# A planned order for GpSimd on the port it shares with VectorE, and another table of stage settings

## The chip, the cores and the metric

One core of a Trainium2 chip. The time is the device time of one execution in microseconds (us). Executions of one kernel agree within about 0.3%. Ratios are the mean time of one kernel's fast runs over that of the kernel before in the same rounds, so they are not quite the ratios of the medians that are quoted beside them. A ratio of 0.99 is 7.8 us.

## The reference

A gated sum of an attention block (32 heads of 16, sequence 2048, width 512) and of a block of two small MLPs:

```python
x = A_x
g = _sigmoid((x * gate_w).sum(-1, keepdims=True))
a = _A_ref(x, A_wqkv, A_wo)              # softmax attention
b = _B_ref(x, B_w1, B_w2, B_w3, B_w4)    # layernorm, GELU, shifted channels; layernorm, GELU
return g * a + (1 - g) * b
```

The exponentials of attention are the bulk: 2048 tiles of 128 x 512.

## The kernel before

The kernel doesn't fix its instruction order by hand. A small model of the engines runs while the program is built (the *planner*); the order in which it starts jobs is the order in which instructions are put into each engine's program. Engines then run freely: each takes its own instructions in order and waits only for data and buffers.

```python
def try_engine(self, e):                      # the planner: engine e is free
    ...
        if any(not self.free[b.cls] for b in j.acq) or j.port and self.lock > self.t:
            continue                          # a job that uses the shared port waits for it
    ...
    self.emit(self.t, j.fn)                   # its place in the program
    self.t_free[e] = self.t + j.hold
    if j.port:
        self.lock = self.t + j.hold           # the port is taken, in the model
```

So the planner knows that VectorE and GpSimd share a port, and never lets two port jobs overlap. But nothing in the program enforced it: the chip could run a GpSimd job earlier against VectorE than planned.

A tile's exponential is made on ScalarE (two tiles in one instruction), or on VectorE with integer arithmetic: one pass from PSUM for each tile, then three shifted copies of a pair of tiles. Two copies usually fall to VectorE, the third to GpSimd:

```python
def sh(k=k):
    d = [b.slot for b in bufs]
    if alone or k == 1 or k == 2 and not both:
        nc.vector.tensor_scalar(out=d[k][:, 0:w], in0=d[0][:, 0:w], scalar1=float(SHIFT * k), scalar2=None,
                                op0=ALU.add)
    else:
        nc.gpsimd.tensor_scalar(out=d[k][:, 0:w], in0=d[0 if both else 2][:, 0:w], scalar1=1.0, ...)
```

A table `STAGES` overrides two dozen settings of the planner for each 32 tiles (how far to look ahead, when VectorE stops taking tiles, how many matmuls fit a gap, `GP2` and `GP3` for the share of copies on GpSimd).

The softmax here doesn't subtract the row's maximum and nothing guards it: scores larger than these inputs give would overflow.

Of the kernel before, what the change touches and what calls it, by code (L numbers as in the profile page):

```python
# [11 lines left out]
ALU = mybir.AluOpType  # L12
# [7 lines left out]
SHIFT = 32  # L20
# [69 lines left out]
class Sim:  # L90
# [45 lines left out]
    def emit(self, t, fn):  # L136
        if fn is not None:
            self.n += 1
            self.order.append((t, self.n, fn))

    def finish_job(self, job):
        job.done = self.t
        self.release(job.frees)

    def try_engine(self, e):
        if self.t_free[e] > self.t:
            return False
        best = None
        for j in self.jobs[e]:
            if j.at > self.tiles:  # L150
                continue
            if j.ready is None:
                if any(d.done is None for d in j.deps):
                    continue
                j.ready = self.t
            if any(not self.free[b.cls] for b in j.acq) or j.port and self.lock > self.t:
                continue
            key = (j.prio, j.ready, j.seq)
            if best is None or key < best[0]:
                best = (key, j)  # L160
        if best is None:
            return False
        j = best[1]
        self.jobs[e].remove(j)
        for b in j.acq:
            self.take(b)
        j.start = self.t
        self.emit(self.t, j.fn)
        self.t_free[e] = self.t + j.hold
        if j.port:  # L170
            self.lock = self.t + j.hold
        self.busy[e] += j.hold
        self.log.append((e, self.t, j.hold, j.name))
        self.push(self.t + j.hold, None)
        self.pending -= 1
        self.push(self.t + j.hold + j.lat, lambda: self.finish_job(j))
        return True
# [57 lines left out]
def kernel(  # L235
# [14 lines left out]
    nc = tc.nc  # L250
# [35 lines left out]
        P1_PRIO=0.414,  # L286
        S_PRIO=0.38,
        GP2=0.0,
        GP3=1.0,
        DVE_STOP=6,  # L290
        DVE_STOP_L=8,
        URG=5,
        URG_L=17,
        DVE_ALONE=2,
        EARLY=68,
        SL=(45, 60),
        IDLE_NS=537,
        PD_LOW=0,
        PA_LOW=0,
        DVE_WAIT=3,  # L300
        AHEAD=9,
        AHEAD2=9,
        PV_FULL=0.916,
        PV_IDLE=0.37,
        PRESS=27,
        MAXU=9,
        ROT=0, DUE_SH=0, AT_SH=0,
    )
    SEG = 32
    STAGES = {0: {'AHEAD': 6, 'EARLY': 13, 'DVE_ALONE': 150, 'S_PRIO': 0.368}, 1: {'AHEAD': 8, 'S_PRIO': 0.415}, 2: {'ROT': 3, 'URG': 3, 'MAXU': 9, 'PD_LOW': 3}, 3: {'PA_LOW': 3, 'DVE_WAIT': 4}, 4: {'SL': (25, 60), 'URG': 2, 'DVE_STOP_L': 9, 'DUE_SH': 40}, 5: {'SL': (25, 60), 'URG': 2, 'DVE_STOP_L': 9, 'DUE_SH': 40}, 6: {'S_PRIO': 0.234}, 7: {'PRESS': 17, 'DVE_WAIT': 5}, 8: {'PV_FULL': 0.776, 'AHEAD': 7, 'PD_LOW': 0}, 9: {'PV_FULL': 0.877, 'ROT': 2, 'AHEAD': 6, 'PA_LOW': 0}, 10: {'PV_FULL': 0.794, 'PA_LOW': 0, 'SL': (165, 60), 'DVE_ALONE': 2}, 11: {'SL': (85, 100), 'EARLY': 62}, 12: {'EARLY': 124, 'PV_IDLE': 0.433, 'DVE_STOP_L': 11, 'SL': (25, 40)}, 13: {'GP3': 0.6, 'DVE_ALONE': 150}, 14: {'ROT': 3, 'GP3': 0.9, 'URG_L': 16, 'AHEAD2': 12}, 15: {'P1_PRIO': 0.309, 'DVE_STOP_L': 5, 'AT_SH': 60, 'DVE_STOP': 5}, 16: {'DVE_WAIT': 2, 'AHEAD2': 10}, 17: {'ROT': 1, 'AT_SH': 10, 'GP3': 0.8, 'DVE_ALONE': 2}, 18: {'P1_PRIO': 0.403, 'GP2': 0.2}, 19: {'PRESS': 10}, 20: {'URG': 7, 'AT_SH': 60, 'GP2': 0.2}, 21: {'IDLE_NS': 352, 'DVE_ALONE': 300}, 22: {'S_PRIO': 0.257}, 23: {'PRESS': 52, 'AT_SH': 60}, 24: {'PA_LOW': 3, 'PRESS': 23, 'GP3': 0.8}, 25: {'PV_IDLE': 0.414, 'AT_SH': 10}, 26: {'DUE_SH': 8, 'PD_LOW': 1, 'GP2': 0.2, 'GP3': 0.9}, 28: {'AHEAD2': 10, 'EARLY': 142}, 29: {'AHEAD': 8, 'S_PRIO': 0.388, 'GP3': 0.9, 'ROT': 1}, 30: {'PV_IDLE': 0.372, 'DUE_SH': -40, 'S_PRIO': 0.412, 'PA_LOW': 2}, 31: {'IDLE_NS': 311, 'GP3': 0.9, 'P1_PRIO': 0.22}, 32: {'DUE_SH': 40, 'DVE_STOP': 5}, 33: {'DVE_STOP_L': 7, 'SL': (205, 60)}, 34: {'P1_PRIO': 0.326, 'PD_LOW': 0, 'PV_IDLE': 0.37, 'GP2': 0.35}, 36: {'PD_LOW': 1, 'DVE_STOP': 7}, 37: {'URG': 4, 'IDLE_NS': 589}, 38: {'ROT': 2}, 39: {'EARLY': 155, 'PA_LOW': 3}, 40: {'DUE_SH': -20, 'PRESS': 8}, 41: {'P1_PRIO': 0.584, 'PA_LOW': 3, 'MAXU': 10}, 42: {'AHEAD2': 8, 'PRESS': 58, 'DVE_ALONE': 0}, 43: {'PD_LOW': 0, 'DVE_WAIT': 2, 'P1_PRIO': 0.216, 'PV_FULL': 1}, 44: {'MAXU': 7, 'ROT': 1}, 45: {'PRESS': 10, 'SL': (65, 80)}, 46: {'DVE_WAIT': 6, 'AT_SH': 120, 'PD_LOW': 0}, 47: {'DUE_SH': 80, 'P1_PRIO': 0.59, 'DVE_ALONE': 150, 'AHEAD2': 6}, 48: {'URG': 8, 'AT_SH': 120}, 49: {'PD_LOW': 3, 'ROT': 3, 'DVE_WAIT': 6, 'AT_SH': 120}, 50: {'DVE_WAIT': 1, 'SL': (5, 60), 'GP2': 0.35, 'DVE_STOP_L': 11}, 51: {'PA_LOW': 3, 'URG_L': 18}, 52: {'ROT': 2, 'PD_LOW': 1, 'PRESS': 35}, 53: {'URG_L': 16, 'IDLE_NS': 245, 'PRESS': 19}, 54: {'PD_LOW': 3}, 56: {'MAXU': 10, 'GP2': 0.1}, 57: {'URG': 2}, 58: {'ROT': 3, 'DVE_WAIT': 5}, 59: {'ROT': 1}, 60: {'GP2': 0.2, 'PV_FULL': 0.879, 'SL': (85, 100)}, 61: {'GP3': 0.6, 'GP2': 0.35, 'PV_FULL': 0.985}, 62: {'GP3': 0.6, 'GP2': 0.35, 'PV_FULL': 0.985}}  # L310
    K = SimpleNamespace(**BASE)


# [11 lines left out]
    def slots(name, n, shape, dt=BF16, where=const):  # L325
# [58 lines left out]
        "den": slots("den", 3, [4, 512], F32, dpool),  # L384
        "rr": slots("rr", 3, [4, 512], F32, dpool),
    })

    def dve(hold, deps, fn, **kw):
        return sim.add(Job("DVE", hold, 280.0, deps, fn, **kw))
# [32 lines left out]
    issue = {"SP": 740.0}  # L422
# [66 lines left out]
    for j in range(4):  # L489
        dma(2200.0, [j_wl], lambda j=j: nc.sync.dma_start(  # L490
            out=woL[32 * j + 1:32 * j + DH + 1, :], in_=A_wo[(25 + 2 * j) * DH:(26 + 2 * j) * DH, :]), prio=5)
# [3 lines left out]
    def warm_pe():  # L495
        for _ in range(11):
# [4 lines left out]
                                                            op0=ALU.bitwise_and), prio=0)  # L501
# [446 lines left out]
    def close_pair(pr):  # L948
        evs["pair"] = None
        evs["n"] = evs.get("n", 0.0) + K.GP2  # L950
        both = evs["n"] >= 1.0
        if both:
            evs["n"] -= 1.0
        rl = pr["pv"][0][0]
        alone = n_left(rl) <= (K.URG_L if rl == NR - 1 else K.URG)
        evs["m"] = evs.get("m", 0.0) + 1.0 - K.GP3
        if evs["m"] >= 1.0:
            evs["m"] -= 1.0
            alone = True
        both = both and not alone  # L960
        w = 512 * pr["h"]
        bufs = [pr["buf"]] + [Buf("PD", pr["h"] + (k == 2)) for k in range(1, 4)]
        pr["buf"].users = pr["h"] + (3 if both or alone else 2)
        bufs[2].users = pr["h"] + (0 if both or alone else 1)
        last = list(pr["jobs"])
        chain = [last]
        for k in range(1, 4):
            def sh(k=k):
                d = [b.slot for b in bufs]
                if alone or k == 1 or k == 2 and not both:  # L970
                    nc.vector.tensor_scalar(out=d[k][:, 0:w], in0=d[0][:, 0:w], scalar1=float(SHIFT * k), scalar2=None,  # L971
                                            op0=ALU.add)
                else:
                    nc.gpsimd.tensor_scalar(out=d[k][:, 0:w], in0=d[0 if both else 2][:, 0:w], scalar1=1.0,  # L974
                                            scalar2=float(SHIFT * (k if both else 1)), op0=ALU.mult, op1=ALU.add)
            if alone or k == 1 or k == 2 and not both:
                j = dve(0.26 * w + 72.0, pr["jobs"], sh, prio=K.S_PRIO, acq=[bufs[k]], frees=[bufs[0]], port=True)
            else:
                j = gp(0.833 * w + 165.0, pr["jobs"] if both else last, sh, prio=1, acq=[bufs[k]],
                       frees=[bufs[0 if both else 2]])  # L980
            if k == 3:
                j.frees.append(pr["token"])
            last = [j]
            chain.append(last)
        for h2, (r2, kt2, i2, G2, p2) in enumerate(pr["pv"]):
            for k in range(4):
                hd = 8 * G2 + 2 * i2 + p2
                V = (lambda kt=kt2, hd=hd: V0[:, kt, hd, :]) if k < 2 else (lambda kt=kt2, hd=hd: V2[:, kt // 2, hd, :])
                add_pv(r2, i2, kt2, V, lambda h2=h2, b=bufs[k]: b.slot[:, h2 * 512:(h2 + 1) * 512].bitcast(BF16),
                       list(chain[k]) + [j_v[kt2, G2 // 2] if k < 2 else j_v2[kt2, G2 // 2]], bufs[k])  # L990
# [371 lines left out]
```

## Time and profile before

782.44 us, the median of 3 runs (782.32 to 783.42).

| in the trace of before | |
|---|---|
| tiles on ScalarE / on VectorE | 1483 / 565 |
| shifted copies on VectorE / on GpSimd | 579 / 270 |
| VectorE instructions on the shared port that took over 60 ns more than usual ("stalls") | 38, 26.2 us too long |
| of these, behind a GpSimd instruction planned *later* ("inverted") | 31, 24.2 us |
| GpSimd jobs that start before the last port instruction of VectorE planned ahead of them has ended | 67 |

How to read it: all three main engines are busy 95% or more, so a busy share says little; what tells is who waits for whom, and whether a wait was planned. The stalls lie inside VectorE's records, which only get longer; the rows of the table come from going through all records and laying the planned order beside them. The lines of the profile are in the prediction. In them, psA and ring are tiles of scores in PSUM, the memory that matmuls write; PA and PD are the exponentials that ScalarE and VectorE make of them; acc is the sum that matmuls build from these.

### The profile page before, as it was taken

To read this page: it belongs to the slowest core of one execution; us is meant where nothing else is said; L and a number is where in the kernel's file an instruction comes from. 1 tells how busy PE (TensorE), PEld (TensorE's weight loads), DVE (VectorE), ACT (ScalarE), POOL (GpSimd) and SP (SyncE) were. 2 spreads that over 40 slices of the span, in tenths; PEclk is the share of its full clock that TensorE was granted. 3 is DMA by queue.
4 is the path that set the end of the run, shared out by engine and by line. 5 is a ranking of instruction groups with operands and counts; after the bars stand their busy time and mean duration, and the time that the engine had idled before them with its cause. 6 is when DMAs were issued, how large, how long until landed. Compare 5 with 4: busy or idle time off the path is not lost.

```text
span 781.1 us, 23746 instructions
## 1 busy us (share of the span) xinstructions
PE 765.1 (98%) x9588; PEld 227.1 (29%) x9588; DVE 740.0 (95%) x1575; ACT 744.4 (95%) x767; POOL 341.5 (44%) x332
## 2 busy tenths in 40 slices
PE   9999999999999999999999999999999999999997
PEld 5333322222222222223232223222223222223222
DVE  6999999999999999998989999999999899999996
ACT  6899999999999999999989999999999999999996
POOL 2255534443344444344345444343454444455531
PEclk9999999999999999999999999999999999999999
DMA  9402133132001221142001001001100000000001
GB/s 191 139 3 37 52 99 84 45 75 86 3 19 33 60 70 39 45 126 50 23 18 33 23 20 47 23 26 25 42 19 20 22 15 26 27 19 20 8 20 40
DMA packets 67093, 34.60 MB, mean 44 GB/s; under 512 B 46748, under 2 KB 62380, under 8 KB 66984
## 3 DMA queue, kind: packets, MB, share of 16 engines
q1 hardware_dynamic: 66040, 32.56, 16.4%
q8 instruction: 75, 1.23, 0.7%
q10 hardware_dynamic: 944, 0.52, 0.2%
q14 instruction: 34, 0.28, 0.1%
HBM read 17.40 MB, written 6.81 MB: 31 GB/s over the span
## 4 chain that ended last, share of the span: by engine, by line
PE 54%; DVE 29%; ACT 10%; issue 4%; DMA 1%; SPq 0%; DVEq 0%; ACTq 0%
PE acc L1005 19%; PE psA L829 17%; PE ring L519 16%; DVE PD L935 12%; DVE PD L971 10%; ACT PA L909 6%; ACT hB L753 2%; ACT hT L753 2%; DVE x_sb L731 1%; DVE st L662 1%; PE ring L829 1%; DVE xn L682 1%; DVE hB L752 1%; DVE accsb L1021 1%; ACT L909 1%
## 5 line engine op out<-in xcount | busy, mean ns | idle before, releaser
L909 ACT ACTIVATE PA<-psA 128x1024 bf16<-128x1024 f32 x742 | 694.5, 1040 | 23.1 <-PE psA L829 8.5
L974 POOL TENSOR_SCALAR PD<-PD 128x1024 uint16<-128x1024 uint16 x270 | 285.1, 1059 | 403.7 <-DVE PD L971 256.6
L935 DVE TENSOR_SCALAR PD<-ring 128x512 uint16<-128x512 f32 x565 | 372.6, 680 | 23.4 <-PE ring L829 21.6
L1005 PE MATMUL acc<-PD,V 128*17 128x512 bf16 x2260 | 308.9, 381 | 3.8 <-DVE PD L971 2.2
L829 PE MATMUL psA<-q,kT 32*128 32x512 bf16 x1483 | 285.7, 384 | 3.8 <-ACT PA L909 3.1
L1005 PE MATMUL acc<-PA,V 128*17 128x512 bf16 x1483 | 278.6, 381 | 0.0
L971 DVE TENSOR_SCALAR PD<-PD 128x1024 uint16<-128x1024 uint16 x579 | 240.2, 453 | 1.1 <-PE acc L1005 0.2
L829 PE MATMUL ring<-q,kT 32*128 32x512 bf16 x565 | 191.6, 384 | 0.9 <-DVE PD L935 0.9
L829 PEld LDWEIGHTS <-kT 32*128 32x128 bf16 x2048 | 75.0, 91 | 306.3 <-issue 304.3
L1005 PEld LDWEIGHTS <-V 128*17 128x17 bf16 x3743 | 75.7, 88 | 140.5 <-issue 118.6
L519 PE MATMUL ring<-xnT,w 128*32 128x512 bf16 x1152 | 88.5, 383 | 0.2 <-DVE PD L935 0.2
L519 PE MATMUL ring<-w,hT 128*32 128x512 bf16 x704 | 58.0, 383 | 0.6 <-DVE PD L935 0.5
L519 PEld LDWEIGHTS <-w 128*32 128x32 bf16 x1920 | 44.7, 95 | 47.0 <-issue 32.9
L1038 POOL TENSOR_TENSOR oT<-accsb,bcs 128x512 bf16<-128x512 f32 x31 | 42.0, 1356 | 9.8 <-DMA bcs<-rr 9.8
L519 PE MATMUL ring<-w,w 128*32 128x256 bf16 (+1 forms) x768 | 41.1, 311 | 0.8 <-DVE PD L935 0.8
L519 PE MATMUL ring<-w,hB 128*32 128x512 bf16 x448 | 36.0, 383 | 0.0
L1021 DVE COPY accsb<-acc 128x512 f32<-128x512 f32 x31 | 21.1, 679 | 0.6 <-PE acc L1005 0.6
L519 PE MATMUL ring<-w,wq 128*32 128x512 bf16 x256 | 20.9, 383 | 0.7 <-DVE PD L935 0.4
L662 DVE BATCH_NORM_STATS2 st<-x_sb 128x6 f32<-128x512 bf16 x32 | 21.5, 678 | 0.0
L519 PEld LDWEIGHTS <-hT 128*32 128x32 bf16 x704 | 15.3, 95 | 21.1 <-issue 16.3
L752 DVE CAST hT<-ring 128x512 bf16<-128x512 f32 x28 | 18.8, 681 | 0.7 <-PE ring L519 0.5
L752 DVE CAST hB<-ring 128x512 bf16<-128x512 f32 x28 | 18.9, 682 | 0.6 <-PE ring L519 0.5
(93 smaller groups left out, 267.1 us busy)
## 6 DMA issues: line engine op xcount, KB each, us to landing
bcs<-rr SPq DMA_DIRECT2D x124, 64.0 KB
xn_dram<-xn SPq DMA_DIRECT2D x32, 128.0 KB
w<-in_B_w_dram SPq DMA_DIRECT2D x5, 512.0 KB
oD<-oT SPq DMA_DIRECT2D x124, 16.0 KB
w<-in_B_w_dram SPq DMA_DIRECT2D x4, 448.0 KB
out_dram<-ot SPq DMA_DIRECT2D x14, 128.0 KB
x_sb<-in_A_x_dram SPq DMA_DIRECT2D x3, 512.0 KB
w<-in_A_wqkv_dram SPq DMA_DIRECT2D x2, 256.0 KB
```

The source lines that it names most:

```text
L519: units.append([Op("col", j, lambda j=j, lf=lf, rf=rf, n0=n0, n1=n1, st=st, sp=sp: nc.tensor.matmul(get()[32 * j:32 * j + 32, n0:n1], lhsT ...
L662: a = dve(600, deps, lambda: nc.vector.bn_stats(out=sb.slot[:], in_=x_sb[:, t, :]), prio=6, at=at, acq=[sb])
L752: pre.append(evac(g, PSUM_NS, lambda ps, m=m: nc.vector.tensor_copy(out=h2()[:, m, :], in_=ps[:])))
L753: ge = act(93 + 427 * FT + 2600, pre, lambda: nc.scalar.activation(out=h2(), in_=h2(), func=ACT.Gelu_apprx_tanh), prio=0)
L829: o = Op("row", i, lambda: nc.tensor.matmul(dst(), lhsT=kT[G][32 * i:32 * i + 32, kt * P:(kt + 1) * P], rhs=qbuf[G, c].slot[32 * i:32 * i ...
L909: job = act(hold, ops, lambda: nc.scalar.activation(out=pb.slot[:, 0:n], in_=buf.slot[:, 0:n], func=ACT.Exp, scale=0.25), acq=[pb], frees= ...
L935: nc.vector.tensor_scalar(out=pr["buf"].slot[:, h * 512:(h + 1) * 512], in0=buf.slot[:], scalar1=BITS_MUL, scalar2=BITS_ADD, op0=ALU.mult, ...
L971: nc.vector.tensor_scalar(out=d[k][:, 0:w], in0=d[0][:, 0:w], scalar1=float(SHIFT * k), scalar2=None, op0=ALU.add)
L974: nc.gpsimd.tensor_scalar(out=d[k][:, 0:w], in0=d[0 if both else 2][:, 0:w], scalar1=1.0, scalar2=float(SHIFT * (k if both else 1)), op0=A ...
L1005: o = Op("col", i, lambda: nc.tensor.matmul(acc[32 * i:32 * i + DH + 1, :], lhsT=lhs(), rhs=rhs(), start=st, stop=True, tile_position=(0, ...
L1021: e = dve(PSUM_NS, round_ops[r], lambda: nc.vector.tensor_copy(out=ab.slot[:], in_=acc[:]), acq=[ab], prio=0)
L1038: n = gp(1250, d3, lambda: nc.gpsimd.tensor_tensor(out=ob.slot[:], in0=ab.slot[:], in1=bb.slot[:], op=ALU.mult), acq=[ob], frees=[ab, bb], ...
```

## The change

The intent: make GpSimd start each job only after the last VectorE port instruction planned before it. Every GpSimd job that has one gets a semaphore wait; VectorE gets none. With it goes another table of settings.

```diff
+    def in_port_order(self, e, fn):
+        def issue():
+            inst = fn()
+            if e == "DVE":
+                self.last_port = inst
+            elif inst is not None and self.last_port is not None:
+                self.tc.add_manual_dep(inst.ins, self.last_port.ins.name, ..., reason="port")
+        return issue
...
-        self.emit(self.t, j.fn)
+        self.emit(self.t, self.in_port_order(e, j.fn) if j.port else j.fn)
...
-    STAGES = {0: {'AHEAD': 6, 'EARLY': 13, 'DVE_ALONE': 150, 'S_PRIO': 0.368}, 1: {...}, ...   # 60 stages, 161 values
+    STAGES = {0: {'DVE_ALONE': 150}, 1: {'GP2': 0.35, 'PRESS': 12, 'SL': (5, 60)}, ...         # 64 stages, 160 values
...
             def sh(k=k): ...                 # now returns the instruction it makes
```

More of the change, by code (lines that the diff above doesn't have):

```diff
@@ L139, in emit @@
             self.order.append((t, self.n, fn))
+    def in_port_order(self, e, fn):
[4 more added lines that the diff above has]
+            elif inst is not None and self.last_port is not None:
+                self.tc.add_manual_dep(inst.ins, self.last_port.ins.name, mybir.DependencyInfo(
+                    mybir.DependencyClass.Sync, mybir.DependencyReason.DATA), reason="port")
+        return issue
     def finish_job(self, job):
@@ L309 @@
     SEG = 32
-    STAGES = {0: {'AHEAD': 6, 'EARLY': 13, 'DVE_ALONE': 150, 'S_PRIO': 0.368}, 1: {'AHEAD': 8, 'S_PRIO': 0.415}, 2: {'ROT': 3, 'URG': 3, 'MAXU': 9, 'PD_LOW': 3}, 3: {'PA_LOW': 3, 'DVE_WAIT': 4}, 4: {'SL': (25, 60), 'URG': 2, 'DVE_STOP_L': 9, 'DUE_SH': 40}, 5: {'SL': (25, 60), 'URG': 2, 'DVE_STOP_L': 9, 'DUE_SH': 40}, 6: {'S_PRIO': 0.234}, 7: {'PRESS': 17, 'DVE_WAIT': 5}, 8: {'PV_FULL': 0.776, 'AHEAD': 7, 'PD_LOW': 0}, 9: {'PV_FULL': 0.877, 'ROT': 2, 'AHEAD': 6, 'PA_LOW': 0}, 10: {'PV_FULL': 0.794, 'PA_LOW': 0, 'SL': (165, 60), 'DVE_ALONE': 2}, 11: {'SL': (85, 100), 'EARLY': 62}, 12: {'EARLY': 124, 'PV_IDLE': 0.433, 'DVE_STOP_L': 11, 'SL': (25, 40)}, 13: {'GP3': 0.6, 'DVE_ALONE': 150}, 14: {'ROT': 3, 'GP3': 0.9, 'URG_L': 16, 'AHEAD2': 12}, 15: {'P1_PRIO': 0.309, 'DVE_STOP_L': 5, 'AT_SH': 60, 'DVE_STOP': 5}, 16: {'DVE_WAIT': 2, 'AHEAD2': 10}, 17: {'ROT': 1, 'AT_SH': 10, 'GP3': 0.8, 'DVE_ALONE': 2}, 18: {'P1_PRIO': 0.403, 'GP2': 0.2}, 19: {'PRESS': 10}, 20: {'URG': 7, 'AT_SH': 60, 'GP2': 0.2}, 21: {'IDLE_NS': 352, 'DVE_ALONE': 300}, 22: {'S_PRIO': 0.257}, 23: {'PRESS': 52, 'AT_SH': 60}, 24: {'PA_LOW': 3, 'PRESS': 23, 'GP3': 0.8}, 25: {'PV_IDLE': 0.414, 'AT_SH': 10}, 26: {'DUE_SH': 8, 'PD_LOW': 1, 'GP2': 0.2, 'GP3': 0.9}, 28: {'AHEAD2': 10, 'EARLY': 142}, 29: {'AHEAD': 8, 'S_PRIO': 0.388, 'GP3': 0.9, 'ROT': 1}, 30: {'PV_IDLE': 0.372, 'DUE_SH': -40, 'S_PRIO': 0.412, 'PA_LOW': 2}, 31: {'IDLE_NS': 311, 'GP3': 0.9, 'P1_PRIO': 0.22}, 32: {'DUE_SH': 40, 'DVE_STOP': 5}, 33: {'DVE_STOP_L': 7, 'SL': (205, 60)}, 34: {'P1_PRIO': 0.326, 'PD_LOW': 0, 'PV_IDLE': 0.37, 'GP2': 0.35}, 36: {'PD_LOW': 1, 'DVE_STOP': 7}, 37: {'URG': 4, 'IDLE_NS': 589}, 38: {'ROT': 2}, 39: {'EARLY': 155, 'PA_LOW': 3}, 40: {'DUE_SH': -20, 'PRESS': 8}, 41: {'P1_PRIO': 0.584, 'PA_LOW': 3, 'MAXU': 10}, 42: {'AHEAD2': 8, 'PRESS': 58, 'DVE_ALONE': 0}, 43: {'PD_LOW': 0, 'DVE_WAIT': 2, 'P1_PRIO': 0.216, 'PV_FULL': 1}, 44: {'MAXU': 7, 'ROT': 1}, 45: {'PRESS': 10, 'SL': (65, 80)}, 46: {'DVE_WAIT': 6, 'AT_SH': 120, 'PD_LOW': 0}, 47: {'DUE_SH': 80, 'P1_PRIO': 0.59, 'DVE_ALONE': 150, 'AHEAD2': 6}, 48: {'URG': 8, 'AT_SH': 120}, 49: {'PD_LOW': 3, 'ROT': 3, 'DVE_WAIT': 6, 'AT_SH': 120}, 50: {'DVE_WAIT': 1, 'SL': (5, 60), 'GP2': 0.35, 'DVE_STOP_L': 11}, 51: {'PA_LOW': 3, 'URG_L': 18}, 52: {'ROT': 2, 'PD_LOW': 1, 'PRESS': 35}, 53: {'URG_L': 16, 'IDLE_NS': 245, 'PRESS': 19}, 54: {'PD_LOW': 3}, 56: {'MAXU': 10, 'GP2': 0.1}, 57: {'URG': 2}, 58: {'ROT': 3, 'DVE_WAIT': 5}, 59: {'ROT': 1}, 60: {'GP2': 0.2, 'PV_FULL': 0.879, 'SL': (85, 100)}, 61: {'GP3': 0.6, 'GP2': 0.35, 'PV_FULL': 0.985}, 62: {'GP3': 0.6, 'GP2': 0.35, 'PV_FULL': 0.985}}
@@ new lines @@
+    STAGES = {0: {'DVE_ALONE': 150}, 1: {'GP2': 0.35, 'PRESS': 12, 'SL': (5, 60)}, 2: {'P1_PRIO': 0.391, 'DUE_SH': 80, 'URG': 7}, 3: {'URG_L': 19, 'GP2': 0.35}, 4: {'GP2': 0.2}, 5: {'SL': (65, 80)}, 6: {'P1_PRIO': 0.23, 'DVE_ALONE': 2, 'SL': (25, 40), 'EARLY': 4}, 7: {'AT_SH': 10, 'DVE_STOP': 4, 'GP2': 0.35, 'P1_PRIO': 0.249}, 8: {'GP2': 0.2, 'PV_FULL': 0.941, 'IDLE_NS': 755}, 9: {'SL': (5, 20), 'EARLY': 113, 'PV_IDLE': 0.548}, 10: {'GP2': 0.2}, 11: {'SL': (165, 180)}, 12: {'PV_FULL': 0.802, 'DUE_SH': 20}, 13: {'S_PRIO': 0.554}, 14: {'PV_FULL': 0.752, 'SL': (85, 100)}, 15: {'IDLE_NS': 519, 'PA_LOW': 0, 'URG_L': 19, 'GP2': 0.2}, 16: {'EARLY': 155, 'DUE_SH': 40}, 17: {'GP2': 0.35, 'PD_LOW': 3}, 18: {'GP2': 0.35, 'MAXU': 11}, 19: {'S_PRIO': 0.349, 'ROT': 1, 'GP3': 0.8}, 20: {'ROT': 1, 'DVE_STOP': 8, 'DVE_ALONE': 0, 'GP3': 0.8}, 21: {'DVE_WAIT': 5, 'PRESS': 8}, 22: {'PD_LOW': 1, 'ROT': 3, 'DVE_STOP_L': 10, 'SL': (85, 60)}, 23: {'URG_L': 20, 'URG': 7, 'AT_SH': 120}, 24: {'IDLE_NS': 835, 'ROT': 2, 'DVE_ALONE': 150}, 25: {'DVE_ALONE': 300}, 26: {'DVE_ALONE': 500, 'PV_FULL': 0.937, 'IDLE_NS': 716}, 27: {'DVE_STOP': 4, 'GP2': 0.2, 'PV_FULL': 0.781, 'DVE_STOP_L': 9}, 28: {'AT_SH': 120, 'PV_FULL': 0.847, 'DUE_SH': 8}, 29: {'URG': 4, 'GP3': 0.8, 'DVE_ALONE': 150}, 30: {'PA_LOW': 2, 'PD_LOW': 0, 'PV_FULL': 0.79, 'GP2': 0.2}, 31: {'ROT': 1}, 32: {'SL': (205, 220)}, 33: {'SL': (205, 220), 'AHEAD2': 11, 'PV_IDLE': 0.391}, 34: {'S_PRIO': 0.546}, 35: {'ROT': 2, 'URG': 8}, 36: {'IDLE_NS': 401, 'P1_PRIO': 0.419}, 37: {'GP2': 0.1}, 38: {'AHEAD2': 12, 'AT_SH': 30, 'ROT': 3}, 39: {'IDLE_NS': 301, 'URG_L': 14, 'AT_SH': 120}, 40: {'GP2': 0.1, 'AHEAD2': 11, 'EARLY': 63, 'S_PRIO': 0.549}, 41: {'GP2': 0.35, 'EARLY': 58, 'PA_LOW': 0}, 42: {'PA_LOW': 3}, 43: {'PRESS': 10, 'DVE_ALONE': 2}, 44: {'ROT': 2}, 45: {'GP3': 0.6, 'S_PRIO': 0.381, 'AT_SH': 30}, 46: {'AT_SH': 120}, 47: {'PRESS': 13, 'AT_SH': 10, 'URG': 8, 'S_PRIO': 0.248}, 49: {'AT_SH': 120, 'DVE_STOP': 7, 'EARLY': 71}, 50: {'PA_LOW': 0, 'AHEAD2': 11, 'DVE_ALONE': 300, 'PD_LOW': 0}, 51: {'GP2': 0.35, 'S_PRIO': 0.435}, 52: {'SL': (85, 60)}, 53: {'DVE_STOP': 7, 'PD_LOW': 2, 'GP2': 0.35}, 54: {'GP3': 0.9, 'AT_SH': 120, 'SL': (65, 60), 'P1_PRIO': 0.31}, 55: {'PA_LOW': 1, 'ROT': 1}, 56: {'GP2': 0.35, 'PA_LOW': 0}, 57: {'P1_PRIO': 0.451, 'DVE_WAIT': 2, 'SL': (65, 80), 'DVE_ALONE': 2}, 58: {'PV_IDLE': 0.477, 'SL': (165, 180), 'PD_LOW': 1}, 59: {'DVE_ALONE': 300}, 60: {'S_PRIO': 0.595, 'GP3': 0.8, 'DVE_STOP': 3, 'AHEAD': 6}, 61: {'PRESS': 11, 'PV_IDLE': 0.427}, 62: {'DVE_STOP_L': 7, 'AHEAD': 10, 'EARLY': 125, 'SL': (65, 80)}, 63: {'PA_LOW': 0, 'SL': (25, 60), 'DVE_STOP_L': 6}, 64: {'AHEAD': 7, 'DVE_WAIT': 1, 'SL': (85, 100)}}
@@ L386 @@
     })
+    sim.tc = tc
+    sim.last_port = None
     def dve(hold, deps, fn, **kw):
@@ L970, in sh @@
                 if alone or k == 1 or k == 2 and not both:
-                    nc.vector.tensor_scalar(out=d[k][:, 0:w], in0=d[0][:, 0:w], scalar1=float(SHIFT * k), scalar2=None,
-                                            op0=ALU.add)
-                else:
-                    nc.gpsimd.tensor_scalar(out=d[k][:, 0:w], in0=d[0 if both else 2][:, 0:w], scalar1=1.0,
-                                            scalar2=float(SHIFT * (k if both else 1)), op0=ALU.mult, op1=ALU.add)
+                    return nc.vector.tensor_scalar(out=d[k][:, 0:w], in0=d[0][:, 0:w], scalar1=float(SHIFT * k),
+                                                   scalar2=None, op0=ALU.add)
+                return nc.gpsimd.tensor_scalar(out=d[k][:, 0:w], in0=d[0 if both else 2][:, 0:w], scalar1=1.0,
+                                               scalar2=float(SHIFT * (k if both else 1)), op0=ALU.mult, op1=ALU.add)
             if alone or k == 1 or k == 2 and not both:
```

## The prediction

> **What bounds the kernel now.** I read four views, from the widest to the narrowest: the engines' busy shares, the chain that ended last, the groups and waits of VectorE and ScalarE, and a stretch of the timeline in which VectorE and GpSimd meet.
>
> The first shows three engines full at once. A step that frees one of them soon runs into another.
>
> ```profile
> PE 765.1 (98%) x9588; PEld 227.1 (29%) x9588; DVE 740.0 (95%) x1575; ACT 744.4 (95%) x767; POOL 341.5 (44%) x332
> ...
> PE 54%; DVE 29%; ACT 10%; issue 4%; DMA 1%; SPq 0%; DVEq 0%; ACTq 0%
> ```
>
> The second line is the chain that ended last. It passes from engine to engine: more than half of it is matmuls, under a third VectorE. A VectorE second is therefore not simply a second of the span; only those in the 29% can be.
>
> The groups give the costs of an exponential. ScalarE makes most of them two tiles at a time (L909). VectorE makes the others with bit arithmetic: a first pass from PSUM (L935), then three shifted copies of a pair of tiles, two usually on VectorE (L971) and the third on GpSimd (L974).
>
> ```profile
> L909 ACT ACTIVATE PA<-psA 128x1024 bf16<-128x1024 f32 x742 | 694.5, 1040 | 23.1 <-PE psA L829 8.5
> L974 POOL TENSOR_SCALAR PD<-PD 128x1024 uint16<-128x1024 uint16 x270 | 285.1, 1059 | 403.7 <-DVE PD L971 256.6
> L935 DVE TENSOR_SCALAR PD<-ring 128x512 uint16<-128x512 f32 x565 | 372.6, 680 | 23.4 <-PE ring L829 21.6
> ...
> L971 DVE TENSOR_SCALAR PD<-PD 128x1024 uint16<-128x1024 uint16 x579 | 240.2, 453 | 1.1 <-PE acc L1005 0.2
> ```
>
> The mean of L971, 453 ns, hides two kinds. The view of that line alone has its spread:
>
> ```profile
> L971 DVE TENSOR_SCALAR PD<-PD x579: 286/418/1502, 12.5 to 770.5; 128x1024 uint16<-128x1024 uint16 x192, 128x512 uint16<-128x512 uint16 x1
> ```
>
> The median is 418 ns and the longest 1502. Where one of the long ones lies, the timeline shows what it met (VectorE's row and GpSimd's of the same stretch):
>
> ```profile
> 199.67 1.27 DVE L971 TENSOR_SCALAR PD<-PD 128x1024 uint16<-128x1024 uint16 x1
> ```
>
> ```profile
> 199.60 1.06 POOL L974 TENSOR_SCALAR PD<-PD 128x1024 uint16<-128x1024 uint16 x1 [1.78 <-DVE PD L971]
> ```
>
> GpSimd started 0.07 us ahead; VectorE's copy took 1.27 us in place of 0.42, and ended 0.28 us after GpSimd's. That is a stall of 0.85 us.
>
> **What the Trainium skill says.** "SBUF — State Buffer", section "Who interferes with whom": VectorE's instructions in a two-port mode, and those with two SBUF inputs against a GpSimd one that reads SBUF, contend with GpSimd for one pair of ports; the one that issues first has it for its whole length and the other waits, and issue order alone decides who. The trace agrees: the pair above, and all stalls found below. The same section says that an instruction with at most one SBUF input outside those modes doesn't contend, and "VectorE: DVE Perf Modes", section "Why PSUM operands drop a tier", that a PSUM operand keeps an instruction out of the two-port modes. So L935 must be immune. It is: 449 of its 565 records overlap a GpSimd instruction, and their mean is 680 ns, the same as the 116 others'.
>
> **The change part by part.** 1. *The order.* Each GpSimd job is made to wait for the last VectorE instruction on the port that the kernel's planner put before it. Nothing is computed anew and no bytes are added. I counted over all records of the seven VectorE groups that use the port those that took over 60 ns more than their group's usual (418 ns for L971, 400 for L682, 340 for L740, 160 for L1029): 38 records, 26.2 us too long in total. Then I laid the planned order of the kernel before beside the trace; it matches instruction by instruction. In 31 of the 38, worth 24.2 us, the blocked VectorE instruction was planned *before* the GpSimd one that blocked it: GpSimd was early, as VectorE ran behind plan. Only 7, worth 2.0 us, were in planned order. The edit forbids exactly the 31. The other way round costs little: GpSimd now waits mostly some 0.5 us in those cases (the 0.07 us of its lead and the 0.42 us of the copy), and it has 403.7 us of idle time before L974.
>
> How much of the 24.2 us is span? Of the 31, 20 lie on VectorE stretches of the chain, 16.5 us: an upper figure, since behind a removed wait another is usually close. A stricter ceiling comes from ScalarE: with the same tiles on it, its 744.4 us of work stay, and only its idle time can shrink.
>
> ```profile
> ACT PA L909 <- PE psA L829: 8.5, 12, 2.4
> ACT PA L909 <- PE acc L1005: 7.8, 15, 2.1
> ...
> ACT PA L909 <- PE ring L829: 4.1, 10, 0.7
> ```
>
> These are 20.4 us in all, nominally waits for TensorE, whose queue in turn waits for VectorE to free a PSUM bank. From the records, the idle time of ScalarE between 20 and 768 us is 21.3 us, and 6.3 us of it lie in gaps that have a stall of VectorE in the 2.5 us before them. The rest has none near: 2.1 us at 401.7 and 1.0 us at 609.4, for instance, where matmuls were late. So the order alone brings some 6 us; I add 1 us, as an estimate, for lag that VectorE carries further than 2.5 us. From it I take 1 us for GpSimd's copies that now land later, which delays matmuls of the third copy. **Order: -6 us.**
>
> 2. *The settings.* The program isn't reordered by hand: the table of settings per 32 tiles steers the planner, so nearly every position moves. What can be counted is the share of shifted copies. GP2 (the second copy goes to GpSimd too) sums to 4.55 over the table, against 2.3. One minus GP3 (VectorE makes all copies) sums to 1.3, against 2.0. There are (579 + 270) / 3 = 283 pairs in 64 stages, 4.4 a stage. So (4.55 - 2.3) x 4.4 = 10 copies go to GpSimd by GP2 and (2.0 - 1.3) x 4.4 = 3 by GP3. VectorE loses 13 copies of 0.34 us (their spacing on the chain, which shows two back to back as 0.67 us), that is 4.4 us; GpSimd gains 13 x 1.06 = 14 us, which it has. If the planner trades the 4.4 us for tiles: one tile on VectorE costs 0.60 us (the chain's spacing of L935) plus two thirds of a pair's three copies, about 0.34 us, so 0.94 us; one less on ScalarE frees 694.5 / 1484 = 0.47 us. With n more tiles on VectorE the sides meet at 4.4 - 0.94 n = 0.47 n, n = 3, and the span falls by 1.5 us. That is what the copies are worth. The other settings (look-ahead, stop limits, matmul slots) have no price in the profile; but a table that was chosen anew was presumably chosen because its plan or its time came out better, which I set at another 1.5 us with a wide margin. **Settings: -3 us.**
>
> Sum: 782.4 - 6 - 3 = 773.4 us.
>
> **The rivals.** *First, TensorE is the bound and hides it.* The chain is 54% matmul, and 11 of the 31 stalls (7.7 us of 24.2) lie where it runs through TensorE. For it: from 484 to 692 us the chain is mostly TensorE. Against: from 184 to 304 us it is mostly VectorE, and most stalls between 85 and 462 us are on it. If it holds everywhere, the order brings 2 us and the time is near 779. *Second, the stalls cost more than ScalarE's near gaps show.* Each lets VectorE fall behind plan, so GpSimd is early again, and PSUM banks come free late for many microseconds. For it: stalls come in groups (189 to 221 us has six). Against: ScalarE's whole mid-run idle time is 21.3 us, so even at half of it the gain is 11 us, and with the settings the time would be near 767. *Third, the new wait takes the place of the old.* GpSimd comes later, then still holds the port when VectorE's next copy, planned after it, arrives; or the third copies land late and TensorE waits. For it: some stalls begin 0.4 to 0.5 us into GpSimd's instruction, where a later start makes them longer. Against: TensorE waits only 2.2 us in all for L971 and 0.2 us for L974, so copies are ready well ahead. It would leave the time at 780 to 785. *Fourth, the settings themselves are worse on the chip* or much better; either moves the time by some 8 us at most, as all three engines are at 95% or more.
>
> **Range and chances.** The middle is 773.4. The first and third rivals bound it above, near 781; the second with good settings bounds it below, near 765. Faster by over 2% needs less than 766.8: the order at half of the idle time and settings worth 5 us, 0.14. Slower by over 2% needs more than 798: no part of the change adds such work, 0.01.
>
> **What would show it.** Right: L971's mean falls from 453 to about 420 ns and its longest records above 1.2 us nearly vanish; VectorE's total excess falls from 26 to under 6 us; GpSimd's instructions of L974 start after the VectorE one planned ahead; ScalarE's mid-run idle time falls to about 14 us; VectorE's share of the chain shrinks and TensorE's grows. L974's count rises to about 283. Wrong: the long copies stay, in planned order now (third rival); or they vanish and ScalarE's waits for TensorE stay at 20 us (first rival); or the counts of L909 and L935 move by more than 15, in which case the settings, and not the port, made the time.

## The result

772.68 us, the median of 4 runs (772.23 to 774.32), against 782.67 (4 runs of before beside it): ratio 0.9875, 95% interval 0.9858 to 0.9892. Some 10 us faster; 773.4 had been predicted.

The page of the kernel after (lines of code are 12 or 13 further down: L922 is the old L909, L948 the old L935, L984 the old L971, L986 the old L974):

```profile
PE 758.8 (98%) x9650; PEld 225.9 (29%) x9650; DVE 723.4 (94%) x1560; ACT 740.9 (96%) x766; POOL 354.6 (46%) x352
...
PE 80%; ACT 14%; issue 2%; DMA 2%; DVE 1%; SPq 0%; ACTq 0%; DVEq 0%
...
L922 ACT ACTIVATE PA<-psA 128x1024 bf16<-128x1024 f32 x741 | 691.0, 1046 | 15.8 <-PE psA L842 6.4
L986 POOL TENSOR_SCALAR PD<-PD 128x1024 uint16<-128x1024 uint16 x290 | 301.9, 1047 | 365.7 <-DVE PD L984 228.2
L948 DVE TENSOR_SCALAR PD<-ring 128x512 uint16<-128x512 f32 x567 | 373.1, 680 | 23.6 <-PE ring L842 21.4
...
L984 DVE TENSOR_SCALAR PD<-PD 128x1024 uint16<-128x1024 uint16 x562 | 222.3, 434 | 1.6 <-PE acc L1017 0.5
```

VectorE's share of the chain fell from 29% to 1%, and TensorE has 80% of it. The copy's mean fell from 453 to 434 ns. The counts of tiles hardly moved (1481 on ScalarE and 567 on VectorE), VectorE makes 17 copies fewer and GpSimd 20 more. No GpSimd job starts ahead of plan any more (67 before), no stall is inverted (31 before). But there are 24 stalls in planned order (VectorE waits for a GpSimd job that was planned ahead of it), 11.7 us, where there had been 7 of 2.0 us.

So total and direction came out as predicted. Whether the *split* did (6 us for the order, 3 for the settings) no single trace can say. That is what the experiments are for.

### The profile page after: what moved, and what is told of

Its sections match the earlier page's. It is cut to its first block, busy times and chain, and to the rows that moved or that the text cites. A ratio compares the mean times of both kernels' runs of the same rounds, so it can differ in the third digit from the quotient of the medians.

```text
span 770.5 us, 23859 instructions
## 1 busy us (share of the span) xinstructions
PE 758.8 (98%) x9650; PEld 225.9 (29%) x9650; DVE 723.4 (94%) x1560; ACT 740.9 (96%) x766; POOL 354.6 (46%) x352
## 4 chain that ended last, share of the span: by engine, by line
PE 80%; ACT 14%; issue 2%; DMA 2%; DVE 1%; SPq 0%; ACTq 0%; DVEq 0%
PE acc L1017 29%; PE psA L842 26%; PE ring L532 23%; ACT PA L922 10%; ACT hT L766 2%; ACT hT L735 1%; DMA pk<-den 1%; ACT hB L766 1%; PE ring L842 1%; ACT L922 1%; DMA xn_dram<-xn 1%; PE ring L510 0%; DVE PD L948 0%; DVE PD L984 0%; PE ring L1295 0%
## 5 line engine op out<-in xcount | busy, mean ns | idle before, releaser
L922 ACT ACTIVATE PA<-psA 128x1024 bf16<-128x1024 f32 x741 | 691.0, 1046 | 15.8 <-PE psA L842 6.4
L986 POOL TENSOR_SCALAR PD<-PD 128x1024 uint16<-128x1024 uint16 x290 | 301.9, 1047 | 365.7 <-DVE PD L984 228.2
L948 DVE TENSOR_SCALAR PD<-ring 128x512 uint16<-128x512 f32 x567 | 373.1, 680 | 23.6 <-PE ring L842 21.4
L1017 PE MATMUL acc<-PD,V 128*17 128x512 bf16 x2268 | 300.7, 381 | 2.6 <-DVE PD L984 2.0
L1017 PE MATMUL acc<-PA,V 128*17 128x512 bf16 x1481 | 273.0, 381 | 0.0
L984 DVE TENSOR_SCALAR PD<-PD 128x1024 uint16<-128x1024 uint16 x562 | 222.3, 434 | 1.6 <-PE acc L1017 0.5
L1017 PEld LDWEIGHTS <-V 128*17 128x17 bf16 x3749 | 73.0, 88 | 131.5 <-issue 112.7
L532 PE MATMUL ring<-xnT,w 128*32 128x512 bf16 x1152 | 92.2, 383 | 0.0
L1050 POOL TENSOR_TENSOR oT<-accsb,bcs 128x512 bf16<-128x512 f32 x31 | 39.5, 1276 | 26.6 <-DVE PD L984 20.6
L675 DVE BATCH_NORM_STATS2 st<-x_sb 128x6 f32<-128x512 bf16 x32 | 21.4, 678 | 0.0
L532 PEld LDWEIGHTS <-hT 128*32 128x32 bf16 x704 | 14.6, 95 | 18.8 <-issue 14.5
L532 PE MATMUL ring<-wo,oD 128*32 128x512 bf16 x224 | 19.8, 384 | 0.0
L532 PE MATMUL ring<-w,wq 128*32 128x512 bf16 x256 | 18.8, 382 | 0.2 <-ACT w L561 0.2
```

Source lines behind the costliest of these rows:

```text
L532: units.append([Op("col", j, lambda j=j, lf=lf, rf=rf, n0=n0, n1=n1, st=st, sp=sp: nc.tensor.matmul(get()[32 * j:32 * j + 32, n0:n1], lhsT ...
L675: a = dve(600, deps, lambda: nc.vector.bn_stats(out=sb.slot[:], in_=x_sb[:, t, :]), prio=6, at=at, acq=[sb])
L922: job = act(hold, ops, lambda: nc.scalar.activation(out=pb.slot[:, 0:n], in_=buf.slot[:, 0:n], func=ACT.Exp, scale=0.25), acq=[pb], frees= ...
L948: nc.vector.tensor_scalar(out=pr["buf"].slot[:, h * 512:(h + 1) * 512], in0=buf.slot[:], scalar1=BITS_MUL, scalar2=BITS_ADD, op0=ALU.mult, ...
L984: return nc.vector.tensor_scalar(out=d[k][:, 0:w], in0=d[0][:, 0:w], scalar1=float(SHIFT * k), scalar2=None, op0=ALU.add)
L986: return nc.gpsimd.tensor_scalar(out=d[k][:, 0:w], in0=d[0 if both else 2][:, 0:w], scalar1=1.0, scalar2=float(SHIFT * (k if both else 1)) ...
```

## The experiments

Theory: the order is worth 6 us because it takes away inverted stalls; the settings are worth 3. Rivals: the settings made the gain; the order is all of it; the settings need the order.

### The two parts, each alone

Edit of `order_only`: the kernel after with the old table. Of `settings_only`: the kernel before with the new table.

```diff
 # order_only                              # settings_only
-    STAGES = <the new table>              -    STAGES = <the old table>
+    STAGES = <the old table>              +    STAGES = <the new table>
```

> The planned order of GpSimd is enforced, the settings stay those of before, so the plan is that of before. My theory (order worth 6 us, settings 3): 776 to 777 us, ratio 0.992 to 0.993; no stall of VectorE behind a GpSimd instruction planned after it (31 and 24.2 us before); some new stalls in planned order (2.0 us before, about 8 now); ScalarE's idle time between 20 us and the tail falls from 21.3 to about 15. Rival A (the new settings made the gain, the order only shifts the stalls): over 780 us, ratio over 0.997, with ScalarE's idle time still near 20 us. Rival B (the order is all of it): 773 us or less.

> The settings of after, no enforced order. My theory: the gain of the settings alone, 3 us, so 779 to 780 us, ratio 0.995 to 0.997, with 20 to 30 us of stalls as before. Rival A (settings made the gain): 773 us. Rival C (the settings were chosen for an enforced order and are worth nothing, or harm, without it): 782 us or more.

Measured in 5 rounds: `order_only` 772.76 us, ratio 0.9859 (0.9845 to 0.9872). `settings_only` 786.66 us, ratio 1.0039 (1.0025 to 1.0053). The order alone gives 1.41%, some 11 us; the settings alone cost 3 us. With the order kept, the new table adds nothing that could be measured (0.9875 against 0.9859, in different jobs, with overlapping intervals). So rival B (the order is all of it) came true, and for the settings alone rival C (worth nothing, or harm, without the order). My split was wrong in both terms, and the errors cancelled.

| trace | stalls, us | inverted | GpSimd ahead of plan | ScalarE idle, us | spacing of activations, us |
|---|---|---|---|---|---|
| before | 38, 26.2 | 31, 24.2 | 67 | 21.3 | 710.6 |
| order_only | 26, 10.3 | 0 | 0 | 15.2 | 699.7 |
| after | 24, 11.7 | 0 | 0 | 14.1 | 699.8 |
| settings_only | 42, 30.7 | 35, 27.6 | 77 | 22.8 | 713.4 |

("Idle" is counted from 20 us to the tail; "spacing" is the sum of the times from one of ScalarE's 735 or so paired exponentials to the next.) The page of `order_only` (before had 744.4 us for ACT):

```profile
PE 759.1 (98%) x9588; PEld 227.9 (30%) x9588; DVE 725.5 (94%) x1575; ACT 739.8 (96%) x767; POOL 334.4 (43%) x332
...
PE 70%; ACT 21%; DVE 5%; issue 3%; ACTq 0%; DVEq 0%
```

ScalarE's idle time fell by 6.1 us with the order, just what I had allowed it. Yet the span fell by more. The last column has the rest: 10.9 us. To see how both can be true, look at ScalarE's timeline of before; each row merges instructions between which no idle time shows:

```profile
198.25 3.77 ACT L909 ACTIVATE PA<-psA 128x1024 bf16<-128x1024 f32 x4
202.41 21.79 ACT L909 ACTIVATE PA<-psA 128x1024 bf16<-128x1024 f32 x23 [0.38 <-PE psA L829]
224.64 24.58 ACT L909 ACTIVATE PA<-psA 128x1024 bf16<-128x1024 f32 x26 [0.45 <-PE ring L829]
249.57 7.48 ACT L909 ACTIVATE PA<-psA 128x1024 bf16<-128x1024 f32 x8 [0.35 <-PE psA L829]
```

and the same work in `order_only`:

```profile
197.03 63.58 ACT L922 ACTIVATE PA<-psA 128x1024 bf16<-128x1024 f32 x69
```

One activation's record is 1.03 us long at the median. In the single row of 69 they start (63.58 - 1.03) / 68 = 0.920 us apart; in the row of 26 before, (24.58 - 1.03) / 25 = 0.942. Records overlap, as the smallest spacing, which nearly half of them have (306 of 735 in before), is 0.904 us. So a delay of up to some 0.12 us makes no gap, and of a longer one 0.12 us is hidden. The Trainium skill says it ("Perfetto Trace Analysis", section "Optimizing Scalar/DVE Operations": an instruction's overhead looks about twice as long in the profile as it keeps the engine busy, since the half that acknowledges the write overlaps with the next instruction); I had not used it. Of the 10.9 us, 6.1 showed as idle time and 4.8 did not.

What the order does is best seen at the stall that the prediction shows. VectorE's three copies and GpSimd's one in before:

```profile
190.69 1.93 DVE L971 TENSOR_SCALAR PD<-PD 128x1024 uint16<-128x1024 uint16 x3
...
199.00 1.94 DVE L971 TENSOR_SCALAR PD<-PD 128x1024 uint16<-128x1024 uint16 x3
```

(two such places), and in `order_only`, in the place of the second, first VectorE, then GpSimd:

```profile
196.86 1.09 DVE L984 TENSOR_SCALAR PD<-PD 128x1024 uint16<-128x1024 uint16 x3
```

```profile
198.13 2.06 POOL L986 TENSOR_SCALAR PD<-PD 128x1024 uint16<-128x1024 uint16 x2 [2.40 <-DVE PD L984]
```

The three copies take 1.09 us in place of 1.94, and GpSimd starts 0.18 us after the third's end.

### Which GpSimd jobs matter

`order_copies` lets only GpSimd's shifted copies wait, `order_rest` only its other jobs (above all the normalising of a finished round), both with the old table:

```diff
-            elif inst is not None and self.last_port is not None:
+            elif fn.__name__ == "sh" and self.last_port is not None:                        # order_copies
+            elif fn.__name__ != "sh" and inst is not None and self.last_port is not None:   # order_rest
```

> Settings of before; only GpSimd's shifted copies wait for the planned VectorE instruction, its other jobs (the normalising of a round, the small ones) don't. In the trace of before, the copies block 16.4 of the 26.2 us of stalls and the others 9.8. If each stall costs alike, this has two thirds of the gain of the order alone: about 4 us, 778 to 779 us. Rival: the copies come early only because a normalising job came early before them, so this alone removes few stalls and gains under 2 us.

> The other half: GpSimd's normalising of a round and its small jobs wait, its shifted copies don't. If each stall costs alike: a third of the gain of the order alone, about 2 us, 780 to 781 us. If the long jobs (1.27 us against 1.05) matter more than their share: as much as the copies. If it gains nothing, the stalls behind normalising were hidden.

Measured: `order_copies` 776.42 us, ratio 0.9906 (0.9893 to 0.992); `order_rest` 778.63 us, 0.9936 (0.9923 to 0.9949). The proportions are about as expected, the sizes twice that. Inverted stalls left: 10.1 us (13) and 13.9 us (18), so 14.1 and 10.3 us were removed, and the gain, 0.94% and 0.64% of 783 us, is 7.4 and 5.0 us. With the whole order it is 24.2 us and 11.0. In all three, about half a microsecond of span for each microsecond of inverted stall (0.52, 0.49, 0.46). Counted against all stalls that went, in planned order too, the ratios scatter more (1.04, 0.64, 0.69; 19.1, 18.4 and 10.3 us of stalls are left). `settings_only` doesn't fit the half: it has only 3.4 us more of inverted stalls, is 3 us slower, and its plan ends 3.1 us earlier; its VectorE also waits 5.5 us for the sums of a round and 2.6 us for the `xn` buffers (0.7 and 0.0 us in before). The rival (copies are early only because a normalising job was) is out: each half works alone, and the halves add up within the intervals (1.58% against 1.41% together). Why a microsecond of inverted stall costs half of one and not all of it, no run tells.

### Is VectorE short of time at all?

Inverted stalls cost VectorE time. A plain reading is that VectorE is short of time and anything that frees it will do; by that reading the new table, with fewer copies on VectorE, should have gained. `stats_free` (from before) and `stats_order` (from `order_only`) free some 15 us of it without touching the order of anything. Their outputs are wrong, which doesn't matter for the times.

```diff
-        a = dve(600, deps, lambda: nc.vector.bn_stats(out=sb.slot[:], in_=x_sb[:, t, :]), ...)
+        a = dve(600, deps, lambda: nc.vector.bn_stats(out=sb.slot[:], in_=x_sb[:, t, 0:64]), ...)
```

> The kernel before, with VectorE's 32 statistics of a row read over 64 elements in place of 512 (a wrong result on purpose: only the time counts). Every instruction keeps its place; VectorE has some 14 us less to do (an estimate: 32 times about 0.45 us of the 0.68 each takes), between 20 and 290 us. In the kernel before VectorE is behind plan there and carries most of the chain from 184 to 304 us: the time should fall by 4 us or more, ratio 0.995 or less. If VectorE was never the bound: ratio 0.998 to 1.

> The same cut in the kernel with the order alone. If with the order kept VectorE is no longer what the span waits for, so that freeing it (as the new settings do) is worth nothing, the time stays within 1 us of the order alone: ratio to before 0.985 to 0.987. If VectorE still bounds it and the new settings failed for another reason: 3 us or more below, ratio 0.982 or less.

Measured: `stats_free` 782.05 us, ratio 0.9984 (0.9969 to 0.9999); `stats_order` 771.89 us, 0.9855 (0.984 to 0.987). The second is as expected: with the order kept, freeing VectorE is worth nothing. The first is a miss. I had expected 4 us or more, since VectorE carries the chain there. The groups of `stats_free` (in before these were 453 ns for the copy, and 21.5 us and 678 ns for the statistics):

```profile
L971 DVE TENSOR_SCALAR PD<-PD 128x1024 uint16<-128x1024 uint16 x579 | 245.0, 462 | 1.1 <-PE acc L1005 0.2
...
L662 DVE BATCH_NORM_STATS2 st<-x_sb 128x6 f32<-128x64 bf16 x32 | 6.5, 212 | 0.0
```

The statistics are 15.0 us shorter, the copies' mean went *up* by 9 ns: the stalls grew from 26.2 to 32.3 us (inverted 24.2 to 28.0). So VectorE's shares of busy time (95%) and of the chain (29%) did not mean that it was short of time. Freeing it by 15 us, at 32 places between 28 and 297 us, brings 1 us; removing 16 us of stalls, all over the span, brought 11.

The kernel's planner gives a yardstick for why. It has a start time for each instruction. This is its own reckoning and no measurement, but the difference to the trace shows where a run falls behind. ScalarE's start in the trace minus the planned one, in us, at six planned times:

| run | 50 | 100 | 200 | 300 | 500 | 755 |
|---|---|---|---|---|---|---|
| before | -0.8 | -0.3 | 0.6 | 3.7 | 6.7 | 8.2 |
| stats_free | -0.8 | 0.4 | 2.3 | 3.4 | 6.0 | 7.5 |
| order_only | -0.2 | -0.7 | -0.6 | -1.3 | -1.4 | -2.1 |
| settings_only | -0.4 | 2.1 | 4.1 | 6.4 | 11.6 | 14.3 |
| after | -0.8 | 0.9 | 1.2 | 0.6 | 0.4 | 0.6 |

Before and `order_only` have the same plan; at the end they are 10.3 us apart, which is the whole difference of their profiled spans (781.1 and 770.9). Without the order, what is lost is scarcely made up again; with it, the chip follows the plan to about 2 us. (Two traces of one kernel, `late` and `late_look` below, are 0.8 us apart at 755, so differences of a microsecond mean little here.) That lost time can't be regained because TensorE is busy in 98% of the span and takes everything in planned order is my reading of it; no run isolates it.

### Does the order pay in an untuned plan?

`plain_free` and `plain_order` are before and after with an empty table.

```diff
-    STAGES = {0: {...}, ...}
+    STAGES = {}
```

> No settings at all (the table is empty), no enforced order: another, untuned plan. It serves as the foot for the next run. I expect it clearly slower than before (over 800 us), with stalls of VectorE of the same kind, most of them behind a GpSimd instruction planned later.

> The same untuned plan with the order enforced. If the order pays in any plan by about 0.7 us for each us of stall that it removes (11.0 us for 15.9 in the tuned plan), the time falls by 0.7 times the difference of the stalls of these two runs, some 5 to 12 us. If it pays only where the settings had been tuned to fill all engines, it gains under 3 us here.

Measured (3 rounds): 824.33 us, ratio 1.0527 (1.0511 to 1.0544), and 813.76 us, 1.0388 (1.0366 to 1.0409). The order pays 1.3% here too, 10.6 us of medians. The settings don't have to be tuned for it. The copies in the traces, `plain_free` and then `plain_order`:

```profile
L971 DVE TENSOR_SCALAR PD<-PD 128x1024 uint16<-128x1024 uint16 x588 | 248.5, 461 | 5.6 <-PE acc L1005 2.6
```

```profile
L984 DVE TENSOR_SCALAR PD<-PD 128x1024 uint16<-128x1024 uint16 x588 | 234.3, 437 | 5.3 <-PE acc L1017 2.3
```

Counted as in the tables above, `plain_free` has 46 stalls of 31.5 us, 29 of them inverted (23.6 us); `plain_order` has 34 of 14.5 us, none inverted. So the order brings 10.6 us for 23.6 us of inverted stalls, 0.45 for each, as in the tuned plan. For all stalls that went, 17.0 us, it is 0.62; 0.7 had been expected. ScalarE is 7.0 us behind its plan at 755 us without the order and 3.7 us ahead with it, 10.7 us apart, nearly all of the 10.9 us between the two spans.

### The order on both sides

`both_ways` is `order_only` with a wait on VectorE as well.

```diff
             if e == "DVE":
                 self.last_port = inst
+                if self.last_gp is not None:
+                    self.tc.add_manual_dep(inst.ins, self.last_gp.ins.name, ..., reason="port")
...
+            if e == "POOL" and inst is not None:
+                self.last_gp = inst
```

> The order alone (settings of before), and VectorE too waits for the GpSimd instruction that the plan puts before its own. It takes no stall away that the order left, since those 26 are in planned order, and it adds a semaphore's way to each. If the order is good only on the engine with idle time: slower than the order alone (ratio 0.986) by 2 to 8 us, ratio 0.988 to 0.996. Rival: a plan kept exactly on both sides is better still, ratio 0.985 or less.

Measured: 774.43 us, ratio 0.9895 (0.988 to 0.991), against 0.9859 (0.9845 to 0.9872) with GpSimd's wait alone; the intervals don't meet. Slower by 0.36%, at the lower edge of what was expected (the two runs are from different jobs, each measured against before). The expectation was wrong on one point: it said that no stall would go. The view of the copies, and VectorE's longest wait for GpSimd:

```profile
L989 DVE TENSOR_SCALAR PD<-PD x579: 286/420/430, 12.5 to 763.4; 128x1024 uint16<-128x1024 uint16 x192, 128x512 uint16<-128x512 uint16 x1
```

```profile
DVE PD L989 <- POOL PD L991: 12.3, 21, 2.1
```

No copy takes more than 430 ns: all 26 stalls of `order_only` (10.3 us) are gone from the records. In their place VectorE waits for GpSimd ahead of its records, 29 times and 15.6 us in all, and ScalarE's spacing is 703.5 us in place of 699.7 (the profiled run was the slowest of the five, by 1.0 us). So waiting by semaphore took longer here than waiting at the port. The wait belongs on the engine with idle time.

### Why the new settings brought nothing

By the planner's own reckoning the new table's plan ends 3.1 us earlier, and my 3 us had happened upon that. The drift table shows where `after` loses: between 50 and 100 us `after` falls behind by 1.7 us while `order_only` gains 0.5, and at 755 us it is 2.7 us worse. The waits of VectorE on transfers in `after`:

```profile
DVE pk L1040 <- DMA pk<-den: 5.3, 7, 1.2
...
DVE xn L695 <- DMA xn_dram<-xn: 1.4, 1, 1.4
```

With the old table there was 0.7 us of the first kind and none of the second. The single wait of 1.4 us lies at 53.86 us, one of 0.90 at 69.66. `late` takes the first kind away, by placing the reciprocal and what follows from it 1.2 us later in the program; `late_third` adds a third buffer for the second, in memory that is idle then.

```diff
+        for j in [r1, r2, d2, *d3, n, *d4]:      # late: reciprocal, transfers, normalising of a round
+            j.late = 1200.0
...
-        self.emit(self.t, ...)
+        self.emit(self.t + j.late, ...)
...
+    xn_bufs = [b[:] for b in sim.free["xn"]] + [hB[:, 0:D]]      # late_third
```

> The kernel after, in which the reciprocal of a round's sums on VectorE, and all that follows from it (a transfer, GpSimd's normalising, the write of the result), stand 1.2 us later in the program; nothing else moves. In the trace of after VectorE waited 5.3 us in 7 places for the transfer that brings these sums, against 0.7 us with the settings of before. If those waits are what ate the expected 3 us of the new settings: they fall below 1 us, and the time falls by 2 to 4 us from after, to 769 to 771 us, ratio to before 0.981 to 0.985. Rival: the new settings simply have no gain to give, since TensorE is on 80% of the chain; then the waits vanish and the time stays within 1 us of after (ratio 0.986 to 0.988).

Measured: 772.43 us, ratio 0.9867 (0.9851 to 0.9883). No gain that stands out. Its trace had not been read then, so one look was taken to see whether the edit had done what it should:

> One look at the kernel of the run named late, whose trace was not kept: VectorE's waits for the transfer of the sums, 5.3 us in 7 places in after, should be below 1 us, while ScalarE's activations stay as far apart as in after (the sum of their spacings within 1 us of 699.8 us), as the time of late (772.4 us) says. If the waits are still there, late tested nothing.

It had (772.35 us, one run). VectorE's longest waits in `late_look`:

```profile
DVE PD L948 <- PE ring L842: 17.1, 45, 1.2
DVE w L561 <- PE ring L552: 4.1, 1, 4.1
DVE hT L765 <- PE ring L532: 2.1, 9, 0.4
DVE xn L695 <- DMA xn_dram<-xn: 2.0, 2, 1.3
```

The 5.3 us are gone, the activations' spacing is 699.5 us (699.8 in `after`), and the stalls in planned order grew from 11.7 to 21.4 us. VectorE's waits only changed their place: 5.3 us fewer for the sums and 4.3 fewer for the ring (17.1 against 21.4), 9.7 us more inside records. The trace of `late` itself agrees: no wait for the sums, 21.9 us of stalls, all in planned order, a spacing of 700.4 us. So ten microseconds more of stalls in planned order did not lengthen the span; but as other waits went at the same time, this doesn't show that they cost nothing.

> The kernel late (settings of after, order kept, sums read 1.2 us later), and a third buffer for the 16 first normalised rows, so that VectorE needn't wait for one of them to be written out (1.4 us at 53.9 us in after, 2.0 us in all in late_look). If the new settings' 3 us were eaten by waits for transfers early on: about 1.3 us below late, 771 us, ratio 0.984 to 0.986, the first version below the order alone, and those waits gone. If not: ratio 0.986 to 0.988 as after and late.

Measured: 772.3 us, ratio 0.9869 (0.9849 to 0.9888). In its trace, one wait of 1.0 us on `xn` is left, and the drift is -1.4 us at 100 and -1.1 at 755, 1.7 us better than `after`; but the profiled run, with a span of 768.8 us against 770.5, was the fastest of the four. The other three took 771.9 to 772.8 us. So it is possible that the early waits took most of the 2.7 us, but neither this trace nor the times show it; where the new table's gain went stays open. No version beats `order_only` beyond the noise.

## Why the prediction was right

**The bound and the stalls: right.** All 31 inverted stalls vanished, and no GpSimd job starts ahead of plan. The copy's mean fell to 434 ns only, not to 420, and 5 records above 1.2 us are left of 19: those in planned order. L935 was immune as said: 680 ns before and after. ScalarE's idle time fell to 14.1 us ("about 14"), VectorE's part of the chain shrank and TensorE's grew, the counts of tiles moved by 2.

**"Order: -6 us": the right mechanism, the wrong size.** It measured 11 us. The step that failed is the "stricter ceiling": that with the same tiles on ScalarE its 744.4 us of work stay and only its idle time can shrink. The busy time is a union of records that overlap; it fell to 739.8 us in `order_only`. The other figure, 16.5 us of stalls on the chain as an upper one, held. Of the rivals the second (stalls cost more than the near gaps show) was right that they do. That it also said 11 us is luck: it took half of ScalarE's idle time, 21.3 us, and that time fell by 6.1. The first (TensorE hides it) is refuted.

**"Settings: -3 us": wrong.** Measured: nothing with the order, 3 us lost without. Two terms failed. The 1.5 us for 13 copies taken off VectorE (17, as measured) supposed that VectorE's time is short; `stats_order` shows that it isn't. The 1.5 us for "a table that was chosen anew" is no argument from the profile, and the chip gave nothing for it. What took it stays open: waits on transfers that the new plan brought early are the candidate, but without them (`late`, `late_third`) the times are the same.

**"Excess under 6 us": wrong.** It was 11.7. The third rival saw this coming: new stalls in planned order did replace some of the old. What the rival had wrong is that the gain would go with it (780 to 785 us).

**The time** was right, 773.4 against 772.68, and would have passed for a confirmation of the split. Two errors of 5 and 3 us had cancelled. The expectations of the first four runs carried the same error on.

## What to carry to other kernels

When a program's order was planned with a model of shared resources, look for the places where the chip's order differs from the plan: here the time followed the waits inside records that invert the plan, about half a microsecond of span for each microsecond in four comparisons, while ten microseconds more of waits that follow the plan did not show in it (`late_look`). Put the enforcing wait on the engine that has idle time, and not on the other as well. And don't take idle time between records as a ceiling for a gain: take the spacing of the starts.

## What the Trainium skill lacked or had wrong

- "SBUF — State Buffer", section "Who interferes with whom", has the lock and that issue order decides, and the trace agrees. It lacks what a stall costs a program: inverted ones about 0.5 us of span for each us (24.2 us cost 11, in the untuned plan 23.6 us cost 10.6). It also says that the loser fully blocks until the first is done; all 32 blocked copies in before ended 0.28 us after GpSimd's record, though one alone takes 0.42 us. So either 0.14 us of a copy isn't held up, or the port comes free before GpSimd's record ends; no run tells which.
- "Perfetto Trace Analysis", section "Optimizing Scalar/DVE Operations", tells that records overlap, but "Optimization Strategy" on the same page sends the reader to the gaps between slices. Here 4.8 of 10.9 us showed in no gap: the records take 1.03 us and the starts are 0.904 us apart at best.
- The same page, section "Identifying the Most-Contended Engine", ranks VectorE, ScalarE and GpSimd by their occupancy. Here that ranking is nearly a tie (ScalarE 744.4 us, VectorE 740.0 us in before), and it says little of what an engine's time is worth: 15 us less work for VectorE brought about 1 us (`stats_free`), none with the order kept (`stats_order`).
- No page that I read has the cost of such an ordering wait: where a GpSimd job was planned for the moment at which the port came free (63 times in `order_only`), it started 0.06 to 0.19 us after the end of VectorE's record, 0.16 at the median. On VectorE's side (`both_ways`) 26 stalls of 10.3 us became 29 waits of 15.6 us.
